# A state space scan followed by an ELU feed-forward block: the last pieces of w_out, the first border's words and the fourth piece of w_in in another order

## The chip, the cores and the metric

The kernel runs on one core of one Trainium2 chip. The core has five engines with instruction queues of their own: TensorE (PE in the profile, with its weight loads shown as PEld), VectorE (DVE), ScalarE (ACT), GpSimd (POOL) and SyncE (SP), which here only starts transfers. Each works through its queue in order, and they wait for one another by semaphores. The metric is the time of one execution on the device, in microseconds (us); the median of several runs counts.

## What is computed

The reference, cut to what matters:

```python
# x (4, 8, 768, 32), a (4, 8, 768), B and C (4, 8, 768, 16); chunks of 32 tokens
cum = np.cumsum(log_a[chunk])
M = (C @ B.T) * exp(cum_i - cum_j) * causal      # per batch and head
y = M @ x + (C @ state) * exp(cum)
state = exp(sum(log_a)) * state + sum_j B_j x_j exp(cum_last - cum_j)
# y of (b, h, s, d) becomes X of (b*s, h*d) = (3072, 256)
h = X @ w_in                                     # (3072, 2048)
g = where(h > 0, h, exp(min(h, 0)) - 1)
out = g @ w_out                                  # (3072, 256)
```

The two weight matrices arrive as 64-bit floating point numbers and are turned into 32-bit ones on the chip; everything else is in 32 bits.

## The kernel before, in words

**Blocks.** The 3072 tokens are twelve blocks of 256, numbered n = 0 to 11. Blocks 0 to 3 are treated one at a time, later ones in pairs (2 and 3 together from the middle of the kernel on, then 4 and 5, and so on). For each block the scan part makes y: `turn_square` and `turn_part` turn B and C (VectorE), `mask_heads` (line 457) makes the masked copies of C, `turn_exp` scales C (VectorE, line 444), `scaled` scales B (GpSimd, line 408), `decay` makes the decay factors (ScalarE, then a select on GpSimd, lines 521 and 526), `scores`, `sums`, `across` and `inside` are small products on TensorE (lines 541, 571, 616, 634), `weigh` and `states` work on their results (VectorE, lines 550 and 588, with a GpSimd product at 593). `inside` ends with copies to `yT` on ScalarE (line 651), in two halves, `ts` 0 and 1.

**Weights.** `pieces` lists sixteen pieces: 0 to 7 are eight column slices of w_in, 8 to 15 are pairs of row slices of w_out. A piece is made by `w_abs` (ScalarE, line 196), `w_low` (ScalarE, line 205, or VectorE, line 209), `w_sign` (VectorE, line 223), `w_high_a` (a clamp on VectorE, line 231), `w_high_b` (VectorE, line 238) and `w_sum` (GpSimd, line 248). `w_high` is the two high steps, `w_take` the first three, `w_give` the others. Pieces are numbered so that w_out's last, 15, is what the eighth step of the second product of block 0 reads, `l2(0, 7)`.

**Products.** Blocks 0 to 3 use full 32-bit products for part of the work: `l1(n, i)` (line 667) for x times w_in, and `l2(n, j)` (line 829) for g times w_out; `elu` follows `l1`. From column slice 8 of blocks 2 and 3 on, `l1_words(n, m)` (line 787) takes three faster passes over words: high words `w1` with `y1`, low words `w0` with `y0`, and sums of words `both_w` with `both_y`. `words_of_w(p)` makes w1 and both_w of piece p on ScalarE and VectorE (lines 736, 737), and `low_of_w(p)` makes w0 on GpSimd (two subtractions, line 845). `words_of_y(n)` makes y1 (lines 755, 757, 759) and y0 (line 762), `both_of_y(n)` makes both_y (line 772, VectorE). After its passes a slice goes through ScalarE (line 793), VectorE (796), ScalarE twice (802, 803, in `begin_end`) and VectorE again (810, in `end_words`, one slice later). `m` counts slices, and slice m reads piece m // 2.

**The second product of pairs.** `second` (line 904) multiplies g by w_out for two blocks with seven products in place of eight. It needs sums of quarters of w_out: `differences` and `sum_weights` make them on GpSimd (lines 845 and 714), `sum_t1` and `sum_t2` make those of g. `differences(i, count)` reads a quarter that `sum_weights` of the same index overwrites.

**Order.** The order of work is written out by hand: an engine's queue holds its instructions in the order of the calls. The stretch that the change touches is, after the first blocks, a loop over j from 0 to 7 (lines 1173 to 1221), in which blocks 2 and 3 take their first slices beside `l2(0, j)` and the last w_out pieces are made (11 at j = 0, 12 to 15 at j = 2 to 5), and a loop over j from 8 to 15, with i = j - 8 (lines 1222 to 1269), in which `l1_words(2, j)` runs beside `l2(1, ...)`. The *first border* is the change from `l1` to `l1_words` at j = 8; the next one is `l1_words(4, 0)`, which follows the second loop. Lines 1270 to 1277 stand between them. PSUM holds seven banks that all these products share (`p_a`) and one more (`p_o`) for `l2` and part of `second`.

The order of the three passes, the one place where the code says more than a sentence:

```python
for ps, lhs, rhs in passes if n > 2 and m == 0 or m == 15 else passes[2:] + passes[:2]:
```

So the sums of words go first, but last for slice 15 and for slice 0 of blocks 4 and later.

Of the kernel before, what the change touches and what calls it, by code (L numbers as in the profile page):

```python
# [32 lines left out]
def kernel(  # L33
# [27 lines left out]
    nc = tc.nc  # L61
# [153 lines left out]
    def w_sign(i, cols=slice(None), eng=nc.vector):  # L215
        if i not in w_sgn:
            w_sgn[i] = ffn.tile([P, 2, CW], U32, tag="g1", name="sgn", bufs=12)
        if eng is nc.gpsimd:
            eng.tensor_scalar(
                out=w_sgn[i][:, :, cols], in0=w_words(i)[1][:, :, cols].bitcast(mybir.dt.int32),  # L220
                scalar1=0.0, scalar2=2.0 ** 31, op0=ALU.is_lt, op1=ALU.mult)
            return
        nc.vector.tensor_scalar(
            out=w_sgn[i][:, :, cols], in0=w_words(i)[1][:, :, cols], scalar1=0x80000000,
            scalar2=None, op0=ALU.bitwise_and)
# [16 lines left out]
    def w_high(i):  # L242
        w_high_a(i)
        w_high_b(i)
# [213 lines left out]
    def mask_heads(n):  # L458
        s = st[n]
        s["ctm"] = att.tile([P, 2, 2, P], F32, tag="ctm", name="ctm")  # L460
        nc.vector.tensor_tensor(
            out=s["ctm"], in0=s["ct"].unsqueeze(2).to_broadcast([P, 2, 2, P]),
            in1=hmask2.unsqueeze(1).unsqueeze(3).to_broadcast([P, 2, 2, P]), op=ALU.mult)
# [218 lines left out]
    def elu():  # L682
        if not begun:
            begin_elu()
        n, i, ps = lag.pop(0)
        e = begun.pop()
        nc.scalar.activation(e, e, ACT.Exp, scale=-1.0)  # L687
        g_of[n, i] = ffn.tile([P, 2, BLK], F32, tag=f"g{n % 2}", name="g", bufs=12)
        nc.vector.scalar_tensor_tensor(
            out=g_of[n, i], in0=e, scalar=1.0, in1=ps,  # L690
            op0=ALU.subtract, op1=ALU.max)
# [39 lines left out]
    def words_of_w(i):  # L731

        w = pieces[i][0]
        k_words[i] = conv.tile(
            [P, 2, KC, CW], F32R, tag="w64", name="w_words", bufs=W_AHEAD)
        nc.scalar.activation(k_words[i][:, 0], w, ACT.Copy, scale=NEAR)
        nc.vector.scalar_tensor_tensor(
            out=k_words[i][:, 1], in0=k_words[i][:, 0].bitcast(F32), scalar=1.0 / WORD - 1.0,
            in1=w, op0=ALU.mult, op1=ALU.add)
# [10 lines left out]
    def words_of_y(n):  # L750

        y = yT[n // 2].rearrange("p k b u i -> p k (b u i)")
        y1 = conv.tile([P, KC, 2 * BLK], F32R, tag="y1", name="y1", bufs=1)
        y0 = conv.tile([P, KC, 2 * BLK], F32R, tag="y0", name="y0", bufs=1)
        nc.scalar.activation(y1[:, 1], y[:, 1], ACT.Copy, scale=NEAR / WORD)
        if n == 4:
            nc.scalar.activation(y1[:, 0], y[:, 0], ACT.Copy, scale=NEAR / WORD)
        else:
            nc.vector.tensor_scalar(
                out=y1[:, 0], in0=y[:, 0], scalar1=NEAR / WORD, scalar2=None, op0=ALU.mult)  # L760
        for k in range(KC):
            nc.vector.scalar_tensor_tensor(  # L762
                out=y0[:, k], in0=y1[:, k].bitcast(F32), scalar=WORD, in1=y[:, k],
                op0=ALU.mult, op1=ALU.subtract)
        y_words[n] = y1, y0

    def both_of_y(n):
        y = yT[n // 2].rearrange("p k b u i -> p k (b u i)")
        y1, y0 = y_words[n]
        both = ffn.tile([P, KC, 2 * BLK], F32R, tag="yT", name="y_both")  # L770
        for k in range(KC):
            nc.vector.scalar_tensor_tensor(  # L772
                out=both[:, k], in0=y1[:, k].bitcast(F32), scalar=1.0 - WORD,
                in1=y[:, k], op0=ALU.mult, op1=ALU.add)
        y_words[n] = y1, y0, both

    def l1_words(n, m, between=None):

        cols = slice(m % 2 * P, (m % 2 + 1) * P)
        w, w0 = k_words[m // 2]  # L780
        w1, both_w, w0 = w[:, 0, :, cols], w[:, 1, :, cols], w0[:, :, cols]
        y1, y0, both_y = y_words[n]
        high, both = psum([P, 2 * BLK], "ps_h"), psum([P, 2 * BLK], "ps_w")
        passes = [(high, w1, y1), (high, w0, y0), (both, both_w, both_y)]
        for ps, lhs, rhs in passes if n > 2 and m == 0 or m == 15 else passes[2:] + passes[:2]:
            for k in range(KC):
                nc.tensor.matmul(  # L787
                    out=ps, lhsT=lhs[:, k], rhs=rhs[:, k], start=k == 0 and lhs is not w0,
                    stop=k == KC - 1 and lhs is not w1)
        if between:  # L790
            words_of_y(between)
        e = ffn.tile([P, 2 * BLK], F32, tag="e", name="e", bufs=2)
        nc.scalar.activation(e, both, ACT.Copy, scale=WORD)  # L793
        if late:
            end_words()
        nc.vector.scalar_tensor_tensor(  # L796
            out=high, in0=high, scalar=WORD - 1.0, in1=e, op0=ALU.mult, op1=ALU.add)
        late.append((n, m, high, e))
# [167 lines left out]
    def w_take(i, low):  # L966

        w_abs(i)
        w_low(i, low)
        w_sign(i)  # L970

    def w_give(i):

        w_high(i)
        w_sum(i)
# [71 lines left out]
    w_abs(3)  # L1047
    w_low(3, nc.scalar)
    w_sign(3)
    mask_heads(1)  # L1050
    w_high(3)
    turn_b(1)
    nc.scalar.activation(F[:, 1], F[:, 0], ACT.Exp)
    write_flat_exp()
# [36 lines left out]
    todo = 5  # L1091
# [77 lines left out]
    def differences(i, count):  # L1169
        for r in range(i, i + count):  # L1170
            sub(s_out[1][:, r], a_out[0][:, r], a_out[2][:, r])

    for j in range(2 * DIRECT):
        n, i = 2 + j // DIRECT, j % DIRECT
        if j < 7:
            l2(0, j)
        piece = todo < len(pieces) and j != 1
        if j == 0:
            elu()
        if piece:  # L1180
            w_take(todo, nc.vector)
        l1(n, i)
        if j == 7:
            l2(0, j)
        if j == 0:
            scaled(3, nc.gpsimd)
            turn(3)
            elu()
            turn_exp(3)
        if piece:  # L1190
            w_give(todo)
            todo += 1
        while lag:
            elu()
        if j == 0:
            decay(3, 2)
            decay(3, 3)
        if j == 1:
            scores(3)
            sums(3)  # L1200
            for q in range(4):
                weigh(3, q)
        if j == 2:
            states(3)
        if j == 3:
            inside(across(3), 3)
        if j == 4:
            words_of_y(2)
        if j == 4:
            words_of_w(4)  # L1210
        if j == 5:
            low_of_w(4)
        if j == 5:
            both_of_y(2)
        scan_ahead(j)
        if j == 3:
            s_out[:] = weight_sums()
        if j == 6:
            differences(0, 4)
        if j == 7:  # L1220
            words_of_w(5)
    for j in range(8, 16):
        i = j - 8
        l1_words(2, j, between=4 if i == 7 else None)
        for p in ((), (6,), (), (7,), (0,), (1,), (2,), ())[i]:
            words_of_w(p)
        for p in ((5,), (), (6,), (7,), (0,), (), (), ())[i]:
            low_of_w(p)
        if i == 7:
            l2(1, 6)  # L1230
            l2(1, 7)
        begin_end()
        if i == 0:
            turn_part(5, 2)
            scaled(4, nc.gpsimd)
            scaled(5, nc.gpsimd)
        if i < 2:
            load_bc(i + 6)
            l2(1, i)
        if i == 2:  # L1240
            turn_part(4, 3)
            turn_part(5, 3)
            scores(4, 5)
            sums(4, 5)
            for q in range(4):
                weigh_two(4, q)
            l2(1, 2)
            states(4)
            states(5)
            for to in (6, 7):  # L1250
                load_b(to)
                spread_cum(to)
        if i == 3:
            l2(1, 3)
        if i == 4:
            y = across(4, 5)
            inside(y, 4, 5, ts=(0,))
            l2(1, 4)
            inside(y, 4, 5, ts=(1,))
        if i == 5:  # L1260
            l2(1, 5)
        if i in (0, 1, 3, 4):
            sum_t1(2, (0, 1, 3, 4).index(i), nc.vector)
        if i in (4, 6):
            turn_part(6, i // 2 - 2)
        if i in (2, 5):
            differences(4 if i == 2 else 6, 2)
        if i < 6:
            sum_weights(nc.gpsimd, a_out, s_out, i)
    both_of_y(4)  # L1270
    end_words()
    words_of_w(3)
    decay(6, 0)
# [107 lines left out]
```

## Time and profile before

| What | Value |
|---|---|
| Time, median of 3 runs | 350.4 us (350.18 to 352.61) |
| Profiled execution, its own time | 349.9 us |
| Its span, from the first to the last instruction | 348.1 us |
| TensorE clock granted, mean | 0.999 |
| TensorE busy, in the stretch from 30 to 80 us | all of it but 0.02 us |
| TensorE busy, from 80 to 88, 88 to 96, 96 to 104, 104 to 112, 112 to 120 us | 7.17, 7.70, 8.00, 7.54, 7.32 of 8 us each |
| VectorE busy, from 88 to 104 us | 15.8 of 16 us |
| GpSimd busy, from 80 to 112 us | 30.6 of 32 us |

The span leaves out 1.8 us of the execution's own time. Times in the text are from the span's start. A row of the timeline has the start of a group of like instructions, how long it lasted, the engine, the line, the operation, what it writes and reads, the shapes and how many there were; in brackets the idle time of the engine before it and what ended that.

### The profile page before, as it was taken

The page shows a single profiled execution, that of the slowest core. Times are in us where ns is not written, and L with a number is a line of the kernel's source. Part 1 is how long each engine was busy: PE and PEld are TensorE (multiplying, and loading weights), DVE is VectorE, ACT ScalarE, POOL GpSimd, SP SyncE. Part 2 cuts the span into 40 slices and gives each one's busy share as a digit, 9 for nine tenths or more (in the row PEclk, how much of TensorE's full clock was granted, in tenths as well). Part 3 has the DMA queues.
Part 4 walks back from the last instruction along what each step waited for, and adds up shares of the span by engine and source line. Part 5 has one row for each costly group of instructions (what it writes and reads, how often), then busy time and mean ns, then how long its engine had stood idle before and what let it go on. Part 6 is the DMA issues. An engine that isn't in the chain of part 4 may idle for free.

```text
span 348.1 us, 9872 instructions
## 1 busy us (share of the span) xinstructions
PE 339.8 (98%) x3878; PEld 297.9 (86%) x3878; DVE 258.7 (74%) x515; ACT 235.3 (68%) x537; POOL 217.1 (62%) x338
## 2 busy tenths in 40 slices
PE   8899999999999999999999999999999999999996
PEld 5679888887777799988988988988988999999995
DVE  3998979879996889775878675888675756665232
ACT  5789989697658889647699447699557566565000
POOL 5654554557999499984196864196854174455760
PEclk9999999999999999999999999999999999999999
DMA  8987979471350321080431070330000100001002
GB/s 135 262 206 166 295 153 263 88 150 45 69 135 8 93 61 33 6 160 7 104 64 32 6 151 15 91 49 2 2 0 5 62 0 3 0 0 62 3 0 62
DMA packets 72727, 26.49 MB, mean 76 GB/s; under 512 B 57768, under 2 KB 67560, under 8 KB 72680
## 3 DMA queue, kind: packets, MB, share of 16 engines
q1 hardware_dynamic: 70360, 25.60, 31.6%
q8 instruction: 30, 0.49, 0.6%
q10 hardware_dynamic: 2320, 0.26, 0.5%
q14 instruction: 17, 0.14, 0.1%
HBM read 22.51 MB, written 3.34 MB: 74 GB/s over the span
## 4 chain that ended last, share of the span: by engine, by line
PE 83%; ACT 4%; DVE 3%; POOL 3%; SPq 2%; issue 2%; DMA 1%; POOLq 0%; DVEq 0%; ACTq 0%
PE ps_o L904 36%; PE ps_h L787 18%; PE ps_w L787 9%; PE ps_h L667 9%; PE ps_o L829 4%; PE ps_y L634 2%; PE ps_g L541 2%; DMA w<-in_moe_w_in_dram 1%; PE ps_y L616 1%; PE ps_st L571 1%; POOL L L526 1%; POOL w L845 1%; ACT e L687 1%; DVE y L762 1%; SPq L178 1%
## 5 line engine op out<-in xcount | busy, mean ns | idle before, releaser
L904 PEld LDWEIGHTS ps_o<-w_out,g 128*128 128x128 f32 x640 | 78.5, 191 | 3.4
L904 PE MATMUL ps_o<-w_out,g 128*128 128x128 f32 x640 | 80.1, 275 | 0.0
L802 ACT ACTIVATE e<-ps_h 128x512 f32<-128x512 f32 x72 | 43.0, 598 | 50.4 <-DVE ps_h L796 50.4
L810 DVE SCALAR_TENSOR_TENSOR g<-e,ps_h 128x512 f32<-128x512 f32 x72 | 49.4, 686 | 30.3 <-ACT e L803 29.8
L845 POOL TENSOR_TENSOR g<-g 128x256 f32<-128x256 f32 x36 | 26.6, 739 | 55.5 <-DVE g L810 55.5
L796 DVE SCALAR_TENSOR_TENSOR ps_h<-ps_h,e 128x512 f32<-128x512 f32 x72 | 50.1, 695 | 13.2 <-ACT e L793 10.1
L793 ACT ACTIVATE e<-ps_w 128x512 f32<-128x512 f32 x72 | 42.3, 588 | 15.0 <-PE ps_w L787 14.9
L787 PE MATMUL ps_w<-y_both,w_words 128*128 128x512 f32 x144 | 51.4, 436 | 0.7 <-DVE y_both L772 0.6
L803 ACT ACTIVATE e<-e 128x512 f32<-128x512 f32 x72 | 45.5, 633 | 2.3
L667 PE MATMUL ps_h<-yT,w_in 128*128 128x256 f32 (+1 forms) x208 | 45.1, 367 | 1.6 <-POOL w_in L248 1.1
L787 PE MATMUL ps_h<-y,w_words 128*128 128x512 f32 x144 | 45.8, 399 | 0.0
L787 PE MATMUL ps_h<-y,w 128*128 128x512 f32 x144 | 44.9, 392 | 0.2 <-POOL w L845 0.2
L667 PEld LDWEIGHTS ps_h<-yT,w_in 128*128 128x128 f32 x208 | 36.4, 190 | 7.2 <-POOL w_in L248 2.3
L521 ACT ACTIVATE L<-L,ncum 128x64 f32<-128x64 f32 x160 | 42.3, 337 | 0.3
L904 PE MATMUL ps_o<-w_sum,g 128*128 128x128 f32 x304 | 38.3, 275 | 0.0
L904 PEld LDWEIGHTS ps_o<-w_sum,g 128*128 128x128 f32 x304 | 37.1, 192 | 1.1
L526 POOL TENSOR_SCALAR_AFFINE_SELECT L<-L 64x512 f32<-64x512 f32 x40 | 29.2, 730 | 9.7 <-ACT L L521 8.3
L787 PEld LDWEIGHTS ps_h<-y,w 128*128 128x128 f32 x144 | 27.0, 188 | 6.9 <-POOL w L845 0.7
L845 POOL TENSOR_TENSOR g<-t,g 128x256 f32<-128x256 f32 x40 | 28.2, 738 | 5.8 <-PE ps_o L904 5.7
L787 PEld LDWEIGHTS ps_h<-y,w_words 128*128 128x128 f32 x144 | 26.4, 188 | 5.9 <-issue 0.5
L829 PE MATMUL ps_o<-w_out,g 128*128 128x256 f32 x128 | 30.6, 383 | 0.8 <-POOL w_out L248 0.8
L845 POOL TENSOR_TENSOR g<-g,t 128x256 f32<-128x256 f32 x40 | 28.8, 754 | 0.2
(133 smaller groups left out, 538.2 us busy)
## 6 DMA issues: line engine op xcount, KB each, us to landing
L<-flat SPq DMA_DIRECT2D x20, 256.0 KB
w<-in_moe_w_out_dram SPq DMA_DIRECT2D x8, 512.0 KB
w<-in_moe_w_in_dram SPq DMA_DIRECT2D x7, 512.0 KB
xr<-in_x_dram SPq DMA_DIRECT2D x24, 128.0 KB
out_dram<-c_sum SPq DMA_DIRECT2D x9, 256.0 KB
bc<-in_B_dram SPq DMA_DIRECT2D x24, 64.0 KB
bc<-in_C_dram SPq DMA_DIRECT2D x22, 64.0 KB
ec<-flat_exp SPq DMA_DIRECT2D x10, 128.0 KB
```

Of the source, the lines that this page charges most:

```text
L521: nc.scalar.activation(L[:, h, u], L[:, h, u], ACT.Exp, bias=ncum[:, u, row:row + 1])
L526: nc.gpsimd.affine_select(out=part, in_=part, pattern=[[0, 4], [0, 2], [1, Q]], compare_op=ALU.is_ge, fill=0.0, base=0, channel_multiplier=-1)
L667: nc.tensor.matmul(out=ps[:, j, toks], lhsT=w_in[i][:, k, j * P:(j + 1) * P], rhs=yT[n // 2][:, k, n % 2].rearrange("p u i -> p (u i)")[:, ...
L787: nc.tensor.matmul(out=ps, lhsT=lhs[:, k], rhs=rhs[:, k], start=k == 0 and lhs is not w0, stop=k == KC - 1 and lhs is not w1)
L793: nc.scalar.activation(e, both, ACT.Copy, scale=WORD)
L796: nc.vector.scalar_tensor_tensor(out=high, in0=high, scalar=WORD - 1.0, in1=e, op0=ALU.mult, op1=ALU.add)
L802: nc.scalar.activation(e, high, ACT.Relu, scale=-1.0)
L803: nc.scalar.activation(e, e, ACT.Exp, scale=-1.0)
L810: nc.vector.scalar_tensor_tensor(out=g_of[n, m].rearrange("p b i -> p (b i)"), in0=e, scalar=1.0, in1=h, op0=ALU.subtract, op1=ALU.max)
L829: nc.tensor.matmul(out=o_of[n][:, ts], lhsT=g_of[n, j][:, m % 2, ts * P:(ts + 1) * P], rhs=w_out[:, m], start=(m == 0 and ts == 0), stop=( ...
L845: nc.gpsimd.tensor_tensor(out=out, in0=in0, in1=in1, op=ALU.subtract)
L904: nc.tensor.matmul(out=ps[:, ts], lhsT=b[:, ts * P:(ts + 1) * P], rhs=a[:, i], start=(i == chunk[0] and ts == 0), stop=(i == chunk[-1]), s ...
```

## The change

`w_high(3)`, the clamp and the second high step of w_in's fourth piece, goes ahead of `mask_heads(1)`. Piece 15 is made at the end of j = 4 in place of j = 5, with its low step on ScalarE in place of VectorE. For blocks 2 and 3 one half of y1 is made by ScalarE in place of VectorE; for blocks 4 and 5 by VectorE in place of ScalarE. Slice 8 takes its sums of words last. The differences of w_out's quarters are spread over i = 0, 2, 3 and 5 in place of j = 6 and i = 2 and 5. `low_of_w(5)` moves from i = 0 to j = 7. The second half of `inside` for blocks 4 and 5 moves from i = 4 to the middle of `l2(1, 5)`. `both_of_y(4)` moves from behind the loop to directly behind `words_of_y(4)`, which is ahead of the ScalarE and VectorE steps of slice 15.

```diff
         nc.scalar.activation(y1[:, 1], y[:, 1], ACT.Copy, scale=NEAR / WORD)
-        if n == 4:
+        if n == 2:
             nc.scalar.activation(y1[:, 0], y[:, 0], ACT.Copy, scale=NEAR / WORD)
         else:
...
-        for ps, lhs, rhs in passes if n > 2 and m == 0 or m == 15 else passes[2:] + passes[:2]:
+        for ps, lhs, rhs in passes if m == (8 if n == 2 else 0) or m == 15 else passes[2:] + passes[:2]:
...
         if between:
             words_of_y(between)
+            if between == 4:
+                both_of_y(4)
...
     w_sign(3)
+    w_high(3)
     mask_heads(1)
-    w_high(3)
     turn_b(1)
...
         while lag:
             elu()
+        if j == 4:
+            w_take(todo, nc.scalar)
+            w_give(todo)
+            todo += 1
...
-        if j == 6:
-            differences(0, 4)
         if j == 7:
             words_of_w(5)
+            low_of_w(5)
...
-        for p in ((5,), (), (6,), (7,), (0,), (), (), ())[i]:
+        for p in ((), (), (6,), (7,), (0,), (), (), ())[i]:
             low_of_w(p)
...
             l2(1, 4)
+        if i == 5:
+            l2(1, 5, half=0)
             inside(y, 4, 5, ts=(1,))
-        if i == 5:
-            l2(1, 5)
+            l2(1, 5, half=1)
...
-        if i in (2, 5):
-            differences(4 if i == 2 else 6, 2)
+        if i in (0, 2, 3, 5):
+            differences((0, 0, 2, 4, 0, 6)[i], 2)
         if i < 6:
             sum_weights(nc.gpsimd, a_out, s_out, i)
-    both_of_y(4)
     end_words()
```

## Prediction before the run

> **What bounds the kernel now.** I read the page's busy shares and its chain first, then the timeline of the weight loads, where TensorE's idle time is given with its releaser, then the other engines' timelines around each idle stretch.
>
> ```profile
> span 348.1 us, 9872 instructions
> PE 339.8 (98%) x3878; PEld 297.9 (86%) x3878; DVE 258.7 (74%) x515; ACT 235.3 (68%) x537; POOL 217.1 (62%) x338
> PE 83%; ACT 4%; DVE 3%; POOL 3%; SPq 2%; issue 2%; DMA 1%; POOLq 0%; DVEq 0%; ACTq 0%
> ```
>
> TensorE is the bound. A reordering that leaves its work as it is can gain no more than its pauses, so I looked for those beside the edits:
>
> ```profile
> 22.53 1.59 PEld L667 LDWEIGHTS ps_h<-yT,w_in 128*128 128x128 f32 x8 [0.65 <-POOL w_in L248]
> 24.45 0.67 PEld L616 LDWEIGHTS ps_y<-bct,Sx 32*64 32x64 f32 x24 [0.33 <-POOL Sx L593]
> ...
> 81.62 1.59 PEld L829 LDWEIGHTS ps_o<-w_out,g 128*128 128x128 f32 x8 [1.23 <-POOL w_out L248]
> ...
> 91.24 0.19 PEld L787 LDWEIGHTS ps_h<-y,w 128*128 128x128 f32 x1 [0.51 <-POOL w L845]
> ...
> 104.95 0.58 PEld L634 LDWEIGHTS ps_y<-M,xr 64*32 64x32 f32 x50 [0.61 <-issue]
> ...
> 116.72 0.19 PEld L787 LDWEIGHTS ps_w<-y_both,w_words 128*128 128x128 f32 x1 [1.01 <-DVE y_both L772]
> 117.32 0.19 PEld L787 LDWEIGHTS ps_w<-y_both,w_words 128*128 128x128 f32 x1 [0.41 <-DVE y_both L772]
> ```
>
> The reader is to see five places, each the consumer of something that the diff moves. From 26 to 80 us and from 118 us on TensorE shows no pause of note.
>
> **The change part by part.** Negative is a gain.
>
> *Piece 15.* l2(0, 7) should follow 16 products of line 667 that begin at 77.17 at 0.216 each, so at 80.63; it begins at 81.62: 0.99 lost to w_sum(15).
>
> ```profile
> 78.36 0.41 DVE L209 TENSOR_SCALAR w_out<-w 128x512 f32<-128x512 uint32 x1
> 80.30 1.27 POOL L248 TENSOR_TENSOR w_out<-mag,w_out 128x512 uint32<-128x512 uint32 x1 [2.88 <-DVE mag L238]
> 80.66 2.58 DVE L772 SCALAR_TENSOR_TENSOR y_both<-y,yT 128x512 fp32r<-128x512 f32 x2
> ```
>
> Moved to j = 4, its steps start behind the elu on VectorE at 73.49: about 74.1 plus sign 0.33, clamp 0.45, shift 0.61 puts w_sum at 75.6 and its end at 76.9, before 80.6. ScalarE gets a low step (0.75) and half of y1 (0.6), 1.35 in all; it has 2.34 us of idle time before its ob copy at 83.65 to hide that. VectorE is relieved of a low step and of y1's half (1.01). Next late would be both_y, which ends at 83.24 while slice 8 begins at 83.27; with y1's second half from ScalarE at 75.8, y0 ends at 77.5, both_y between 80.5 and 81.7, and slice 8 now reads it last, after 82.8. So the 0.99 goes whole: -0.99.
>
> *low_of_w(5) and the differences.* Slice 10 waits for w0 of piece 5: its second low pass begins 0.63 after the first, and what follows 0.43 after that (91.67), where such steps take 0.23: 0.60 lost. GpSimd did four differences (2.16) and a select ahead. Now low_of_w(5) follows the select directly and ends near 88.5, where TensorE asks after 90: -0.60. The differences cost GpSimd the same 2.16, later, two by two (0.9 to 1.3); it starts that stretch some 2.8 earlier, so its sums still end by 113.7. Price at nothing; if that cover were gone, each pair would put 0.9 on low_of_w(7), which ends at 105.35 for a slice at 108.67.
>
> *inside, second half.* It pauses after 13 of 64 at 104.28 and goes on at 104.95; the small products come at 0.007 each, so 0.6 is lost, with no semaphore behind it. Between the two halves lay 1.73 us of l2; now lie 1.73 of l2, a slice (1.4) and half of l2 (0.87). Bounds 0 (the pause moves along) and -0.6; I take -0.6, since the later borders, with 1.98 between the halves, show none.
>
> *both_y(4).* Slice (4, 0) has its high passes done at 115.98 and leaves at 117.66, with 0.47 of work: 1.2 lost, 1.1 without the usual start-up. -1.1 if both_y comes in time.
>
> Sum of TensorE's pauses: 0.99 + 0.60 + 0.60 + 1.1 = 3.3. Two things are late next.
>
> *First border.* ScalarE's order there is unchanged, and VectorE's elu at 21.48 waits for it, so the states, their product Sx and `across` at 24.45 can't come sooner: the 0.65 ahead of l1(0, 3) turns into waiting at 24.45. Gain 0. It can lose:
>
> ```profile
> 18.58 0.81 POOL L408 TENSOR_TENSOR sc<-bc,eb 128x256 f32<-128x256 f32 x1
> 18.83 1.11 DVE L461 TENSOR_TENSOR ctm<-bct,hmask 128x512 f32<-128x512 f32 x1
> 20.92 0.42 DVE L444 TENSOR_TENSOR bct<-bct,ec 128x256 f32<-128x256 f32 x1
> 21.15 1.33 POOL L248 TENSOR_TENSOR w_in<-mag,w_in 128x512 uint32<-128x512 uint32 x1 [1.76 <-DVE mag L238]
> ```
>
> The masked copies took 1.11 beside `sc`, 0.68 elsewhere: 0.43 lost to an operation of GpSimd. In the new order w_sum(3) becomes ready during the masked copies and takes 1.28 just as turn_exp is due; turn_exp ran ahead of it before. Ends: 0, and 1.0 (turn_exp from 20.9 to 22.5, elu at 22.46 in place of 21.48). I take the 0.43 of the one row less the 0.14 that VectorE is free between turn_exp's end at 21.34 and the elu: +0.3, carried through 26 to 80, where nothing absorbs it.
>
> *The words of y for block 4.* The net shift into the second loop is s = 0.99 - 0.3 = 0.7.
>
> ```profile
> 105.66 1.15 ACT L651 COPY yT<-ps_y 128x256 f32<-128x256 f32 x3 [0.31 <-PE ps_y L634]
> 106.83 0.60 ACT L793 ACTIVATE e<-ps_w 128x512 f32<-128x512 f32 x1
> ...
> 117.28 0.61 ACT L736 ACTIVATE w_words<-w_in 128x512 fp32r<-128x512 f32 x1
> ```
> ```profile
> 111.77 0.64 DVE L453 STREAM_TRANSPOSE bct<-bc 128x256 f32<-128x256 f32 x1
> 113.58 1.29 DVE L762 SCALAR_TENSOR_TENSOR y<-y,yT 128x512 fp32r<-128x512 f32 x2 [1.17 <-ACT y L757]
> 115.38 0.69 DVE L796 SCALAR_TENSOR_TENSOR ps_h<-ps_h,e 128x512 f32<-128x512 f32 x1
> 115.98 1.28 DVE L772 SCALAR_TENSOR_TENSOR y_both<-y,yT 128x512 fp32r<-128x512 f32 x2
> ```
>
> VectorE is full from 88 to 105 and moves with s. The yT copies no longer hold back slice 13 on ScalarE, but slice 14; all less s: the first half's copies to 105.3, line 793 to 105.85, VectorE's 796 at 105.95 (it was 107.46), lines 802 and 803 to 107.8, the second half's copies (1.15) to 108.95, line 793 to 109.5, line 796 of slice 14, words of piece 2 and the transpose (0.6 each) to 111.35, where it was 112.41. From there y1's half, two y0, two both_y and one end_words lie ahead of slice 15's step of line 796. Uncontended they take 0.33 + 1.2 + 1.2 + 0.6 = 3.3, contended (1.01, 1.75, 1.6) 5.0; I take 4.3, as GpSimd runs only short sums (0.46) there. Line 796 then starts at 115.65 - s, against 115.38: 0.43 sooner. Behind it are queued lines 802 and 803, words_of_w(3) on ScalarE, and low_of_w(3), (1), (2) on GpSimd. The fourth of those six subtractions ended at 121.79 and what follows slice (4, 2)'s last pass began at 123.08; loaded as late as possible, as at 91.24, that pass could have let it begin at 121.84 + 0.43 = 122.27. That leaves 0.8 of slack. So TensorE can gain 0.8 + 0.43 = 1.2 there, whatever it gained before: of 3.3 - 0.3 = 3.0, another 1.8 turns into a wait at slice (4, 2).
>
> Sum: -1.2. On the profiled execution's own 349.9 that is 348.7; the median of the runs shown is 0.5 above it, so 349.2.
>
> **The rivals.** (a) *Every pause goes.* No loss at the first border (s = 1.0) and line 796 at 114.7 - s: 0.8 + 0.68 + 1.0 = 2.5, so 347.9. For it: turn_exp ran unhindered beside the start of w_sum. Against: VectorE's rows of 0.85 to 1.2 next to GpSimd. 0.20.
>
> (b) *The first border costs its whole 1.0.* GpSimd, waiting since mid-mask, goes first, and turn_exp stands behind a whole w_sum. Then s = 0, line 796 is at 115.65, and the gain is 0.8 - 0.27 = 0.5: 349.9. For it: the two both_y at 80.66 took 2.58 in place of 1.28, as if taking turns with w_sum(15) and low_of_w(4). Against: one row only, of 0.43. 0.20.
> The Trainium skill says this outright (SBUF — State Buffer, "SBUF: two separate sides"): VectorE with two operands in SBUF and GpSimd reading SBUF share a port pair by exclusive lock, held for the whole instruction. The trace agrees as far as the 1.11 beside 0.68; that GpSimd wins the pair here, no run shows. By that rule alone the time would be that of this rival.
>
> (c) *PSUM holds slice 13 back, and it is slower.* The second half of `inside` now keeps two banks through l1_words(2, 13). If that slice gets the banks that the first half's yT copies free, at 105.36 - s, it starts at 104.7, not 102.7; behind it come a slice, l2's halves and `inside` (1.5 + 0.87 + 1.4 + 0.87), so slice 14 starts at 109.3 in place of 108.67. Its high product ends at 110.8; from there line 796 of slice 14, the words of piece 2 and the transpose (1.9) and the 4.3 put line 796 of slice 15 at 117.0, 1.6 later, and slice (4, 2) loses 1.6 - 0.8 = 0.8: 351.2. It decides once line 796 is later than 116.2. For it: before, slice 13 began at 105.62, after those copies, so the trace can't exclude it. Against: slices 11 and 12 free two banks sooner (by 102.4). 0.12.
>
> **How the numbers follow.** The forecast has 0.42, (a) 0.20, (b) 0.20, (c) 0.12; 0.06 is left for what I did not see, on both sides. The forecast's own range is 348.0 to 350.3 (the ends of line 796, 114.7 - s and 116.3 - s, with s between 0.2 and 0.9). The range for 8 in 10 is 347.5 to 350.9: it takes in (b) and most of (a), and stops short of (c). About 1%, 3.5 us, is what a measurement of this kernel can tell from no change. A gain of that size exceeds all pauses (3.3), and only the worst end of (c) with a loss at the first border comes near the other side: faster 0.05, same 0.90, slower 0.05.
>
> **What would show it.** Right: no idle at l2(0, 7), at slice 10's w0 or in `inside`; l1(0, 3) starting near 22.2 and `across` waiting for Sx until 24.7 or so; a new wait of TensorE on GpSimd's line 845 at slice (4, 2). Wrong: `across` at 24.45 or before (then (a)), turn_exp longer than 1 us (then (b)), an idle stretch ahead of slice 13 (then (c)), or no wait at (4, 2), which would say that the last step of this sum is too strict.

## The result, and the profile after

The changed kernel takes 351.3 us (median of 22 runs, 350.79 to 352.16) against 350.34 (22 runs, 349.12 to 352.61): a ratio of 1.0028, 95% interval 1.0018 to 1.0037. That is 0.96 us slower, where a gain of 1.2 was forecast, and it lies above the predicted range, 347.5 to 350.9. It is less than the 1% that the prediction set as the least that can be told from no change; the interval of 22 runs on either side tells 0.28% from no change, so that bound was too coarse. The profiled execution has a time of its own of 350.81 us.

The page after, the same three lines:

```profile
span 349.1 us, 9876 instructions
PE 339.0 (97%) x3878; PEld 297.6 (85%) x3878; DVE 259.3 (74%) x514; ACT 235.1 (67%) x538; POOL 220.0 (63%) x338
PE 77%; ACT 8%; DVE 7%; SPq 2%; issue 2%; DMA 2%; POOL 1%; DVEq 0%; POOLq 0%; ACTq 0%
```

TensorE does the same work, but holds 77% of the chain in place of 83%; ScalarE and VectorE have risen. The timeline of TensorE after, at the places that the prediction looked at and wherever it waited next (the line numbers quoted from 793 on are 2 higher than before):

```profile
23.34 1.97 PE L667 MATMUL ps_h<-yT,w_in 128*128 128x256 f32 x8 [0.90 <-DVE g L689]
25.41 0.88 PE L616 MATMUL ps_y<-bct,Sx 32*64 32x64 f32 x24
...
81.45 1.89 PE L831 MATMUL ps_o<-w_out,g 128*128 128x256 f32 x8
...
92.50 0.85 PE L571 MATMUL ps_st<-xr,b_tok 64*32 64x64 f32 x48 [0.41 <-POOL w_sum L847]
...
120.78 0.49 PE L787 MATMUL ps_h<-y,w 128*128 128x512 f32 x1 [0.28 <-POOL w L847]
121.91 0.50 PE L787 MATMUL ps_h<-y,w 128*128 128x512 f32 x1 [0.63 <-POOL w L847]
...
146.00 0.84 PE L571 MATMUL ps_st<-xr,b_tok 64*32 64x64 f32 x56 [0.43 <-DVE c_sum L884]
```

The reader is to see: `l2(0, 7)` at 81.45 without a wait, and slice 10 and `inside` without one too. `across` is at 25.41 in place of 24.45. The pause at slice (4, 0), 1.01 and 0.41 on the weight loads before, is 0.50 once on them, and too short for a mark on the products. New are 0.41 at `sums` of blocks 4 and 5 (GpSimd's differences), 0.28 and 0.63 at slice (4, 2), and 0.43 at `sums` of blocks 6 and 7, which wait for VectorE.

**How executions are compared.** Single executions start unevenly: `w_abs(2)` (line 196 on ScalarE), the first step that waits for the transfer of piece 2, begins between 14.56 and 16.10 us in the profiles of this case. So below I count places in a profile from that start. Of the 0.96 by which `across` is later in the rows above, 0.39 is such a late start (14.96 for 14.57). Two profiles of the kernel before then agree within 0.2 us at the places of the next table; between 105 and 116 us they differ by 0.4.

### The profile page after: what moved, and what is told of

The parts are those of the page before. It is cut to its first block, busy times and chain, and to the rows that moved or that the text cites. A ratio compares the mean times of both kernels' runs of the same rounds, so it can differ in the third digit from the quotient of the medians.

```text
span 349.1 us, 9876 instructions
## 1 busy us (share of the span) xinstructions
PE 339.0 (97%) x3878; PEld 297.6 (85%) x3878; DVE 259.3 (74%) x514; ACT 235.1 (67%) x538; POOL 220.0 (63%) x338
## 3 DMA queue, kind: packets, MB, share of 16 engines
HBM read 22.51 MB, written 3.34 MB: 74 GB/s over the span
## 4 chain that ended last, share of the span: by engine, by line
PE 77%; ACT 8%; DVE 7%; SPq 2%; issue 2%; DMA 2%; POOL 1%; DVEq 0%; POOLq 0%; ACTq 0%
PE ps_o L906 31%; PE ps_h L787 15%; PE ps_h L667 10%; PE ps_w L787 8%; PE ps_o L831 5%; PE ps_y L634 2%; DVE ps_h L798 2%; ACT L L521 2%; DMA w<-in_moe_w_in_dram 2%; ACT e L804 2%; PE ps_y L616 2%; ACT e L805 1%; PE ps_st L571 1%; ACT e L795 1%; PE ps_g L541 1%
## 5 line engine op out<-in xcount | busy, mean ns | idle before, releaser
L847 POOL TENSOR_TENSOR g<-g 128x256 f32<-128x256 f32 x36 | 27.3, 757 | 56.0 <-DVE g L812 55.9
L526 POOL TENSOR_SCALAR_AFFINE_SELECT L<-L 64x512 f32<-64x512 f32 x40 | 29.9, 746 | 9.9 <-ACT L L521 8.5
```

Source lines behind the costliest of these rows:

```text
L526: nc.gpsimd.affine_select(out=part, in_=part, pattern=[[0, 4], [0, 2], [1, Q]], compare_op=ALU.is_ge, fill=0.0, base=0, channel_multiplier=-1)
L847: nc.gpsimd.tensor_tensor(out=out, in0=in0, in1=in1, op=ALU.subtract)
```

## The experiments

The theories, as the expectations name them. *W*: the prediction's own, `low_of_w(1)` at slice (4, 2) sets the end. *V*: from slice 15 on VectorE's queue, with ScalarE's, sets the pace, and what goes ahead of line 798 there is paid. *Q*: the loss is there by 25 us, from the transfer of piece 2 on. *P*: it lies in late pauses, and at the last store. *L*: `turn_exp` is shut out for as long as one instruction of GpSimd runs; *N* is anything else at that place. *First border* in the prediction and below is the stretch from 19 to 25 us, from block 0 to block 1 (not the change from `l1` to `l1_words`).

All results in one table. Places are in us from the start of `w_abs(2)`, of one profile each; "end" is the stretch from the start of the last product to the end of the span; "DVE" is the number of instructions on VectorE, semaphore instructions counted.

| Kernel | Median, us | Ratio to before, 95% interval | DVE | turn_exp | across | 796/798 of slice 15 | last product | end |
|---|---|---|---|---|---|---|---|---|
| before | 350.34 | 1 | 707 | 0.42 | 9.89 | 100.81 | 329.97 | 3.60 |
| ctl_before | one run | | 707 | 0.42 | 9.70 | 100.71 | 330.08 | 3.41 |
| after | 351.30 | 1.0028 (1.0018 to 1.0037) | 706 | 1.32 | 10.46 | 100.50 | 330.03 | 4.09 |
| ctl_after | one run | | 706 | 1.31 | 10.44 | 100.53 | 329.70 | 4.46 |
| before_border | 351.30 | 1.0022 (1.0010 to 1.0034) | 708 | 1.31 | 10.55 | 101.50 | 330.85 | 3.34 |
| after_border_back | 350.65 | 0.9999 (0.9984 to 1.0014) | 705 | 0.43 | | | | 3.48 |
| after_sum_halves | 350.71 | 1.0016 (1.0006 to 1.0027) | 706 | 0.77 | 9.90 | 99.94 | 329.49 | 4.20 |
| after_y_back | 350.33 | 0.9994 (0.9980 to 1.0008) | 705 | 1.31 | 10.45 | 99.56 | 329.76 | 3.50 |
| both_back | 349.07 | 0.9960 (0.9945 to 0.9974) | 704 | 0.42 | 9.72 | 98.57 | 328.62 | 3.27 |
| border_order_back | 348.51 | 0.9950 (0.9938 to 0.9961) | 705 | 0.42 | 9.70 | 98.04 | 328.11 | 3.50 |
| border_order_back_w3 | 349.50 | 0.9972 (0.9960 to 0.9985) | 705 | 0.42 | 9.67 | 98.02 | 328.94 | 3.49 |
| after_w3 | 350.51 | 1.0003 (0.9993 to 1.0013) | 706 | 1.31 | 10.44 | 100.61 | 329.89 | 4.08 |
| after_three_sets | 350.37 | 0.9991 (0.9979 to 1.0004) | 708 | 1.31 | 10.45 | 100.58 | 329.84 | 3.31 |
| border_order_back_two_sets | 349.74 | 0.9969 (0.9955 to 0.9983) | 706 | 0.42 | 9.70 | 98.04 | 328.09 | 4.08 |
| grid_neither | 348.50 | 0.9920 (0.9908 to 0.9932) | 708 | 0.42 | 9.72 | 98.10 | 327.91 | 3.34 |
| grid_border | 349.24 | 0.9948 (0.9935 to 0.9961) | 708 | 1.31 | 10.46 | 98.85 | 328.65 | 3.36 |
| grid_y | 349.32 | 0.9952 (0.9940 to 0.9964) | 708 | 0.42 | 9.80 | 99.84 | 329.09 | 3.56 |
| grid_both | 350.72 | 0.9995 (0.9982 to 1.0009) | 708 | 1.31 | 10.44 | 100.57 | 329.69 | 3.46 |

The profile of after_border_back was taken at a granted clock of 0.994, so its places are left out. Each group of runs had its own runs of the kernel before beside it, and their medians go from 350.32 to 351.08. So a ratio is to the kernel before of the same group, and medians from different groups can't be compared to better than some 0.8 us. The groups are: before and after; the next row with after_border_back, after_y_back and both_back; after_sum_halves with border_order_back, its w3 version and after_w3; the two "sets"; and the four of the grid.

### The first border

`before_border`, the swap alone, in the kernel before:

```diff
+    w_high(3)
     mask_heads(1)
-    w_high(3)
```

> The kernel before, with only the clamp and shift of w_in's fourth piece put ahead of the masked copies. Theory V: turn_exp waits for w_sum and takes 1.3, across comes 0.7 later, TensorE is 0.7 later up to 80 us and slice 15's step starts near 116.1 in place of 115.38: 351.0, 0.7 over the kernel before. Theories Q and P: 350.3, no change.

`after_border_back`, the swap taken out of the changed kernel:

> The changed kernel, with the clamp and shift of w_in's fourth piece back behind the masked copies. Theory V (VectorE's queue): turn_exp runs in 0.42 again in place of 1.31, the states and across come 0.7 sooner, slice 15's step after its passes (line 798 there) starts near 114.8 in place of 115.46, and all behind it moves along: 350.6, 0.7 under the changed kernel's 351.3. Theory Q (the late first border comes from a late transfer of piece 2 in the one profiled execution): no change, 351.3. Theory P (the loss is TensorE's short pauses late in the kernel, at 145, 205 and 213, and the last store): no change, 351.3.

The swap alone costs 0.22% (0.8 us), and the last product comes 0.8 to 0.9 us later, counted from a step by which the transfer of piece 2 has landed: it is the swap's own loss, and not a late transfer's, as Q would have it. In the changed kernel, taking it out gains 0.29% (0.9999 for 1.0028), about 1.0 us; as its end is 0.6 to 1.0 shorter (below), this run alone doesn't show the border's share. VectorE's timeline after, and GpSimd's:

```profile
19.10 0.75 DVE L231 TENSOR_SCALAR mag<-mag 128x512 f32<-128x512 f32 x1
19.89 0.69 DVE L238 SCALAR_TENSOR_TENSOR mag<-mag,sgn 128x512 uint32<-128x512 uint32 x1
20.50 0.68 DVE L461 TENSOR_TENSOR ctm<-bct,hmask 128x512 f32<-128x512 f32 x1
21.29 1.32 DVE L444 TENSOR_TENSOR bct<-bct,ec 128x256 f32<-128x256 f32 x1
22.52 0.67 DVE L689 SCALAR_TENSOR_TENSOR g<-e,ps_h 128x512 f32<-128x512 f32 x1
```
```profile
20.73 1.59 POOL L248 TENSOR_TENSOR w_in<-mag,w_in 128x512 uint32<-128x512 uint32 x1 [1.15 <-DVE mag L238]
```

`turn_exp` (line 444) takes 1.32 in place of 0.42: `w_sum(3)` began while the masked copies ran (20.50 to 21.18), and `turn_exp` ends 0.29 behind its end (22.61 and 22.32). The elu comes at 22.52 in place of 21.48, and TensorE's `l1(0, 3)` waits for it. To tell whether that is one instruction's length, `after_sum_halves` splits the sum:

```diff
-    w_sum(3)
+    w_sum(3, ks=slice(0, 1))
+    w_sum(3, ks=slice(1, 2))
```

> The changed kernel, with w_sum(3) on GpSimd made in two halves of 0.65 in place of one operation of 1.28. Theory L (turn_exp, with both operands in SBUF, is shut out while one GpSimd instruction runs): VectorE gets in between the halves, turn_exp takes 0.7 or so in place of 1.31, across comes 0.6 sooner, and the time falls by 0.6: 350.7, ratio 1.0011. Rival N (turn_exp is late for another reason, or GpSimd keeps its turn through both halves): turn_exp still takes 1.3 or more, ratio 1.0028.

```profile
21.38 0.77 DVE L444 TENSOR_TENSOR bct<-bct,ec 128x256 f32<-128x256 f32 x1
```
```profile
20.82 1.92 POOL L248 TENSOR_TENSOR w_in<-mag,w_in 128x256 uint32<-128x256 uint32 x2 [1.15 <-DVE mag L238]
```

`turn_exp` now ends at 22.15, before GpSimd's second half does (22.74) and 0.28 behind the end of its first half (21.87), as it ended 0.29 behind the whole sum above. `across` is 0.56 sooner (9.90 for 10.46). So it is shut out for one instruction of GpSimd at a time: L. The Trainium skill states this (SBUF — State Buffer, "SBUF: two separate sides": the shared port pair is an exclusive lock, held for the whole instruction by whichever started first), and the 1.32, 0.77 and 0.42 agree. That GpSimd, which was already waiting, got in ahead of `turn_exp` is what these runs add.

### The words of y for block 4

`after_y_back` puts `both_of_y(4)` back behind the loop, and block 4's half of y1 back on ScalarE; `both_back` undoes the border as well:

```diff
-        if n == 2:
+        if n in (2, 4):
...
-            if between == 4:
-                both_of_y(4)
...
+    both_of_y(4)
     end_words()
```

> The changed kernel, with the words of y for block 4 as before: both halves of y1 on ScalarE, and the sums of words of y behind the loop, so behind slice 15's step. Theory V: slice 15's step starts near 114.0 in place of 115.46; TensorE waits about 1.2 for the sums of words at slice (4, 0), but no longer 1.35 at slice (4, 2); VectorE's queue is 1.4 earlier from there on and TensorE no longer waits at the sums of blocks 6 and 7: 350.3 to 350.7, 0.6 to 1.0 under the changed kernel. Theory P: 351.3.

> The changed kernel with both of these put back: the fourth piece's clamp and shift behind the masked copies, and the words of y for block 4 as before. Theory V: the two gains add, slice 15's step near 113.3: 349.5 to 350.0, below the kernel before by 0.3 to 0.8. Theory Q: as the version with the words of y alone. Theory P: 351.3.

after_y_back has 350.33 (0.9994), in the range that V gave, but not for V's reason alone. Line 796 of slice 15 comes 0.9 sooner (99.56 for 100.50, where 1.5 was expected), and the waits at slice (4, 2) and at the sums of blocks 6 and 7 are gone. Yet its last product, at 329.76, is 0.27 sooner than in one profile of the changed kernel and 0.06 later than in the other, while its end is 0.6 to 1.0 shorter: most of what its time gained lies at the end. both_back, at 349.07 (0.9960), gained more than expected; its last product is 1.1 to 1.4 sooner than the changed kernel's.

`border_order_back` is both_back with y1's half left on VectorE, so that only the two orders are undone. `border_order_back_w3` calls `words_of_w(3)` at i = 7 on top of that, and `after_w3` does so in the changed kernel:

```diff
-        for p in ((), (6,), (), (7,), (0,), (1,), (2,), ())[i]:
+        for p in ((), (6,), (), (7,), (0,), (1,), (2,), (3,))[i]:
             words_of_w(p)
...
     end_words()
-    words_of_w(3)
```

> The changed kernel with the first border put back, and the sums of words of y for block 4 put back behind the loop, but y1's first half for block 4 left on VectorE. It parts the two edits that went back together in the version at 0.996. Theory V: VectorE starts y0 0.8 sooner than in that version, where it waited 1.22 for ScalarE's y1; slice 15's step and the sums of words each come some 0.6 sooner: ratio 0.994, 0.6 us under that version. Rival: the half on VectorE costs what the wait did; ratio 0.996.

> The same, and words_of_w(3) called at i = 7, ahead of slice 15's last steps on ScalarE, in place of behind the loop. Theory V (VectorE and ScalarE pace each other from slice 15 on): ScalarE's queue is 0.5 shorter there, at most 0.5 of gain: ratio 0.993 to 0.994. Theory W (the prediction's: low_of_w(1) on GpSimd, which follows words_of_w(3), sets the end at slice (4, 2)): no wait is left at (4, 2) in the version without this edit, so no gain: ratio as that one.

> The changed kernel, with words_of_w(3) called at i = 7, so that low_of_w(3), (1) and (2) start 2 us or more sooner. Both theories: TensorE's wait of 1.35 at slice (4, 2) goes. Theory W: that wait was what ate the gain, so the time falls by about 1.3: 350.0, ratio 0.999. Theory V: TensorE is stopped later by VectorE's queue (at the sums of blocks 6 and 7, 0.6), which gains only the 0.5 that ScalarE is rid of: 350.8, ratio 1.0014.

With both orders undone the rest of the change gains 0.40 to 0.50%: border_order_back, at 0.9950, beats both kernels. Against both_back its line 796 of slice 15 and its last product are 0.5 sooner (98.04 for 98.57, 328.11 for 328.62), as V expected of y1's half on VectorE; the two ratios, of different groups, don't tell them apart.

after_w3 has 1.0003, between what W and V expected, so the time doesn't decide. Its profile does: it has no wait at slice (4, 2) any more, but its last product comes at 329.89, where the changed kernel's two profiles have 330.03 and 329.70. The wait turned up later, most of it at the sums of blocks 6 and 7 (145.97, 0.58 of TensorE's idle time, for a result of VectorE). So W is out: the wait at (4, 2) isn't the last limit.

border_order_back_w3 missed both expectations: V had a gain, W no change, and the last product came 0.8 later. Line 796 of slice 15 is where it was (98.02 for 98.04); the extra word step of VectorE delays both_y instead, and TensorE's pause for it at slice (4, 0) goes from 0.38 to 1.19. So VectorE's time was paid there too, but through both_y and not, as V has it, through the step of slice 15.

### The end of the program

The changed kernel's last product, so counted, came no later than before, yet the medians differ by 0.96. Two second profiles:

> The kernel before, unchanged, for a second profile of it. Read from the start of w_abs(2) on ScalarE (line 196, the first step that waits for piece 2's transfer), the first profile had `across` at 9.89 us, line 796 of slice 15 at 100.81 and the last product at 329.97. If single profiles read in this way can be trusted to 0.3 us, this one has 9.6 to 10.2, 100.5 to 101.1 and 329.7 to 330.3. If they scatter as much as the kernels differ, the last is off by 0.6 or more.

> The changed kernel, unchanged, for a second profile of it. Read in the same way the first profile had `across` at 10.46 us, line 798 of slice 15 at 100.50 and the last product at 330.03, that is only 0.06 later than the kernel before, where the medians say 0.96. If the difference is scatter of the two single profiles, this one has its last product at 330.6 to 331.2. If it lies behind the last product (the last store) or ahead of w_abs(2), the last product comes at 329.8 to 330.3 again, and the span beyond it is longer than that of the kernel before by some 0.5.

The last product comes at 329.70, and the rest takes 4.46 (4.09 in the first profile), against 3.60 and 3.41 before: the changed kernel loses 0.5 to 1.0 us behind its last product. In the records of the transfers, the last load of instructions (queue 14) begins 1.8 and 2.2 us behind the last product's start, within the last store; before it is at 1.1 and 0.9. In all profiles the place of that load, and the end, went by the number of instructions on VectorE, which the change had altered by one. So I altered that number alone, at 1.05 us, where VectorE has idle time behind it; `after_three_sets`:

```diff
-    nc.vector.memset(keep, 1.0)
+    nc.vector.memset(keep[:, 0, 0:64], 1.0)
+    nc.vector.memset(keep[:, 0, 64:128], 1.0)
+    nc.vector.memset(keep[:, 1], 1.0)
```

> The changed kernel, but the memset of line 272 on VectorE (at 1.05 us, with 1.8 us of idle time behind it) in three parts, so VectorE's queue is two instructions longer and nothing else is moved. In all profiles so far the stretch from the start of the last product to the end of the span went by the number of instructions on VectorE, semaphore instructions counted: 707 or 708, 3.35 to 3.60 us (the kernel before among them); 706, 4.08 to 4.46 (the changed kernel, twice, and two of its variants); 704 or 705, 3.27 to 3.50. In the same profiles a load of instructions (queue 14) lies at 0.9 to 1.1 us behind that start, at 1.8 to 2.2, within the last store, or at 3.8 to 4.1. Theory T (the load of VectorE's last block of instructions holds up the last store where the two meet): with 708 the stretch takes 3.3 to 3.6 again, and the time is 0.5 to 0.8 lower than the changed kernel's 351.3: 350.5 to 350.8, a ratio of 1.0005 to 1.0015. The rival (the longer end has to do with the change itself, or is chance): 4.1 to 4.5 again, and 351.3.

`border_order_back_two_sets` does the same in two parts, `keep[:, 0]` and `keep[:, 1]`:

> The version that has been the fastest (border and both_of_y(4) in their old order), but the memset of line 272 in two parts: one instruction more on VectorE, 706 in place of 705. Theory T: the load of instructions falls on the last store, the stretch behind the last product's start takes 4.1 to 4.5 in place of 3.5, and the time rises from 348.5 by 0.6 to 0.9: a ratio of 0.997 in place of 0.995. The rival: 3.5 and 0.995 again.

The end went from 4.09 and 4.46 to 3.31, and from 3.50 to 4.08, as expected of theory T. It holds in all 18 profiles: with 706 instructions the end takes 4.08 to 4.46 (five profiles), with 704, 705, 707 or 708 it takes 3.27 to 3.60 (thirteen). The last packet of the store (queue 1) is over 2.50 to 2.87 behind the last product's start in the five, and 1.90 to 2.12 in the others. The last store's issue, in the SyncE timelines after, of after_three_sets, of border_order_back and of its two_sets version, each under the answer's own line with the span:

```profile
core 0 of [0], span 349.1 us
...
345.68 0.35 SPq L898 DMA_DIRECT2D out_dram<-c_sum  x1
```
```profile
core 0 of [0], span 347.8 us
...
345.20 0.35 SPq L900 DMA_DIRECT2D out_dram<-c_sum  x1
```
```profile
core 0 of [0], span 346.7 us
...
343.92 0.35 SPq L896 DMA_DIRECT2D out_dram<-c_sum  x1
```
```profile
core 0 of [0], span 346.7 us
...
343.35 0.35 SPq L897 DMA_DIRECT2D out_dram<-c_sum  x1
```

From issue to end: 3.4, 2.6, 2.8 and 3.35. And the transfers behind that issue after (the window from 346.6 to 348.6):

```profile
q1 hardware_dynamic: 124, 0.06, 9.6%
q14 instruction: 1, 0.01, 1.7%
```

The store's packets and one load of instructions share that window; in after_three_sets both late loads are over by then, and its window from 346.2 to 347.6 has queue 1 alone. The Trainium skill (Runtime: NRT & Kernel Launch, "Instruction fetch mechanics") has instruction fetch hidden behind the issuing of instructions, and speaks there of the engine's own issue and not of other transfers; here the end was 0.6 to 1.2 us longer where a load met the last store. Theory P, which looked to the last store, was right in this part. That the load delays the store is an inference from both tests; what in the load does it isn't shown.

The times fit in part: border_order_back_two_sets has 0.9969 (expected 0.997); after_three_sets has 0.9991, lower than expected (1.0005 to 1.0015). These are ratios of different groups of runs, so the two orders are measured side by side below, with ends alike.

### Two by two

Four kernels in one group, all brought to 708 instructions on VectorE (the memset in three or four parts): with both parts, with only `both_of_y(4)` early, with only the swap at the border, and with neither. The rest of the change is in all four.

> The changed kernel with VectorE's queue brought to 708 instructions (the memset of line 272 in three parts), so that its end can be compared with the other three of this group, brought to the same number: a two-by-two of the two parts that were found to cost time, with the difference at the end of the program taken out. This one has both parts. From its first measurement: a ratio of 0.9991, between 0.998 and 1.0005. Theory A (the two losses add): 0.2 to 0.35 per cent above each of the two with one part. Theory M (each of them alone makes a limit, and the larger of the two counts): the same as the one with both_of_y(4) early alone.

> w_high(3) behind mask_heads(1) as before, both_of_y(4) early as in the changed kernel, 708 instructions on VectorE. Theory A: 0.9965 to 0.998, with the border's loss of 0.2 to 0.35 per cent gone from the one with both. Theory M: the same as with both, 0.9985 to 1.0005, TensorE arriving sooner at slice (4, 2) and waiting there for longer.

> w_high(3) ahead of mask_heads(1) as in the changed kernel, both_of_y(4) behind the loop as before, 708 instructions on VectorE. Theory A: 0.996 to 0.998. Theory M: 0.9975 to 0.9995, the loss of 0.3 per cent at the first border above the one with neither part, and within 0.1 per cent of the one with both.

> Both parts in their old order, the rest of the change kept, 708 instructions on VectorE. Both theories: 0.9945 to 0.996, as measured with 705. That is the gain of the rest of the change, 1.4 to 1.9 us.

Above "neither", the border adds 0.74 us and the words of y 0.82, both together 2.2 (medians); by the last product 0.74, 1.18 and 1.78. The sum of the two single losses is 1.56 by the medians and 1.92 by the last product, so they add, roughly, as theory A says, and M, by which the words of y alone would cost as much as both, is out. The ratios themselves missed both theories: the three versions that lack a part came 0.1 to 0.3% lower than either had them, and the gap between both parts and one is 0.43 to 0.47%, where A had 0.2 to 0.35. In the profiles the border's loss is there from `across` on and stays (0.74 at both ends). TensorE's waits in grid_neither, then in grid_y, from 76 to 150 us:

```profile
92.33 0.85 PE L574 MATMUL ps_st<-xr,b_tok 64*32 64x64 f32 x48 [0.42 <-POOL w_sum L848]
114.91 0.50 PE L790 MATMUL ps_w<-y_both,w_words 128*128 128x512 f32 x1 [0.31 <-DVE y_both L775]
115.77 0.50 PE L790 MATMUL ps_w<-y_both,w_words 128*128 128x512 f32 x1 [0.36 <-DVE y_both L775]
```
```profile
92.18 0.85 PE L574 MATMUL ps_st<-xr,b_tok 64*32 64x64 f32 x48 [0.41 <-POOL w_sum L850]
120.45 0.50 PE L790 MATMUL ps_h<-y,w 128*128 128x512 f32 x1 [0.28 <-POOL w L850]
121.59 0.51 PE L790 MATMUL ps_h<-y,w 128*128 128x512 f32 x1 [0.63 <-POOL w L850]
145.69 0.84 PE L574 MATMUL ps_st<-xr,b_tok 64*32 64x64 f32 x56 [0.44 <-DVE c_sum L887]
```

The waits for both_y at slice (4, 0), 0.67 together, go in grid_y, and three others come, 1.35 together. VectorE's timelines of the two, up to the step of slice 15 (line 799, then 801, the 796 of before):

```profile
111.16 1.89 DVE L765 SCALAR_TENSOR_TENSOR y<-y,yT 128x512 fp32r<-128x512 f32 x2
112.98 0.68 DVE L813 SCALAR_TENSOR_TENSOR g<-e,ps_h 128x512 f32<-128x512 f32 x1
113.57 0.69 DVE L799 SCALAR_TENSOR_TENSOR ps_h<-ps_h,e 128x512 f32<-128x512 f32 x1
114.17 1.54 DVE L775 SCALAR_TENSOR_TENSOR y_both<-y,yT 128x512 fp32r<-128x512 f32 x2
```
```profile
110.98 1.89 DVE L765 SCALAR_TENSOR_TENSOR y<-y,yT 128x512 fp32r<-128x512 f32 x2
112.80 1.81 DVE L775 SCALAR_TENSOR_TENSOR y_both<-y,yT 128x512 fp32r<-128x512 f32 x2
114.53 0.68 DVE L815 SCALAR_TENSOR_TENSOR g<-e,ps_h 128x512 f32<-128x512 f32 x1
115.12 0.69 DVE L801 SCALAR_TENSOR_TENSOR ps_h<-ps_h,e 128x512 f32<-128x512 f32 x1
117.14 0.69 DVE L815 SCALAR_TENSOR_TENSOR g<-e,ps_h 128x512 f32<-128x512 f32 x1 [1.33 <-ACT e L808]
```

Moving both_y ahead buys TensorE 0.92 (its end: 100.24, then 99.32) and pushes the step of slice 15 back by 1.74 (98.10, then 99.84). Behind that step stands a ring in which VectorE and ScalarE wait for each other. In grid_y VectorE waits for ScalarE's line 808 six times between 115 and 145 us (0.25 to 1.33), and ScalarE for VectorE's line 801 seven times (0.27 to 1.76). The last rounds of it, and the adds to `c_sum` for which TensorE waits at the sums of blocks 6 and 7, first in grid_y, with a row of ScalarE, then in grid_neither:

```profile
143.26 0.69 DVE L815 SCALAR_TENSOR_TENSOR g<-e,ps_h 128x512 f32<-128x512 f32 x1 [1.07 <-ACT e L808]
144.80 0.74 DVE L887 TENSOR_TENSOR c_sum<-ps_o,c_sum 128x256 f32<-128x256 f32 x2
```
```profile
144.59 0.60 ACT L807 ACTIVATE e<-ps_h 128x512 f32<-128x512 f32 x1 [0.95 <-DVE ps_h L801]
```
```profile
143.42 0.74 DVE L885 TENSOR_TENSOR c_sum<-ps_o,c_sum 128x256 f32<-128x256 f32 x2
```

Counted from `w_abs(2)` (15.28 and 15.48 in these two profiles) the adds start at 129.52 and 127.94: of the 1.74 at slice 15, 1.58 is still there 30 us later. TensorE shows no wait between 122 and 145 us, so it isn't TensorE that holds the ring up.

## Why the prediction was wrong, step by step

How far TensorE is ahead of the kernel before (mean of its two profiles, counted from `w_abs(2)`) at the start of what is named, in us; negative is sooner, and "after" is the first profile of the changed kernel:

| Place (time before) | neither | border | y | both | after |
|---|---|---|---|---|---|
| across (24.6) | -0.04 | +0.71 | +0.05 | +0.69 | +0.71 |
| l2(0, 7) (81.6) | -1.17 | -0.41 | -1.13 | -0.41 | -0.48 |
| slice 10, second low pass (91.2) | -1.76 | -1.00 | -1.72 | -1.02 | -1.07 |
| sums of 4 and 5, behind their wait (93.0) | -1.57 | -0.81 | -1.54 | -0.82 | -0.88 |
| slice (4, 0), second pass over both_y (117.3) | -2.41 | -1.66 | -3.32 | -2.60 | -2.67 |
| slice (4, 2), behind its wait (122.8) | -2.38 | -1.64 | -1.93 | -1.21 | -1.28 |
| sums of 6 and 7, behind their wait (146.0) | -2.29 | -1.54 | -1.04 | -0.32 | -0.39 |
| a product of blocks 10 and 11 (308.9) | -2.14 | -1.40 | -0.91 | -0.31 | -0.02 |

- *Piece 15 (0.99) and low_of_w(5) (0.60)*: right in place and about in size, 1.1 and 0.6 (first column). The differences, priced at nothing, cost 0.2 at the sums of 4 and 5, where the row after names one of them as what ended the wait.
- *inside (0.60)*: the pause is gone, but its size was one execution's: between the same two products the second profile of before has 0.37 in place of 0.67. Nor are this pause and the next one separate terms: in that profile TensorE waits 0.29 longer for both_y at slice (4, 0) (0.87 for 0.58 on the products).
- *First border (+0.3)*: **mis-sized**. It cost 0.74, and rival (b)'s mechanism was right: GpSimd, waiting during the masked copies, goes first, and `turn_exp` stands behind what is left of w_sum. I took the one row with 0.43 (a VectorE step beside `sc`) less 0.14 of slack, and not the whole instruction that was about to start.
- *l1(0, 3) near 22.2*: wrong. It was at 23.34, as its first product waits for an elu, which stands behind `turn_exp`.
- *Words of y, line 796 sooner by 0.43*: a consequence of s. With s = 1.17 - 0.74 = 0.43, and not 0.7, the same sum (115.65 - s) gives 0.16 sooner; it came 0.2 sooner (100.50 to 100.58 for 100.76). What I put between the transpose and line 796 (4.3, of bounds 3.3 and 5.0) is 4.5 after (110.95 to 115.46).
- *The cap of 1.2 at slice (4, 2)*: right in its mechanism, and in its number partly by luck. TensorE was 2.6 ahead and is 1.2 to 1.3 ahead behind that wait. But line 796 was 0.2 sooner and not 0.43, and the slack behind it was 1.0 to 1.1 and not 0.8; the two errors cancel.
- *That the 1.2 then lasts to the end*: **the step that failed**. I followed the delay to the first consumer with slack, and not on through VectorE's and ScalarE's ring. VectorE was only 0.2 ahead, and where TensorE next waits for a result of that queue, at the sums of blocks 6 and 7, the lead shrinks from 1.2 to between 0.3 and 0.4: the step put at nothing cost 0.9. The order of before leaves 1.2 us more at that point: the pause of 1.1 at (4, 0) was the price of a queue that is in time later.
- *The end of the program*: a term put at nothing, as the prediction stops at slice (4, 2). It cost 0.5 to 1.0 by the profiles.

Together: the last product is level with before in one profile after and 0.33 ahead in the other; the first loses 0.26 in a pause at 213.49 that the other lacks and for which no releaser is named. The end of the span, counted from `w_abs(2)`, is 334.11 and 334.16 in the two profiles after, 333.57 and 333.49 before: 0.6 slower, of the 0.96 measured. The other 0.4 is ahead of that step or is scatter of single profiles; no run tells which. Rival (b) had the border right, but its 349.9 shares the last two errors. Rival (a) is out, since the waits came back; so is (c), as TensorE is busy for all of the 16 us from 96 to 112 after.

What stays open: ratios of different groups scatter more than their intervals say. The version with neither part has 0.9950 with 705 instructions and 0.9920 with 708, at ends and last products that agree within 0.2 us. Its own medians agree too, 348.51 and 348.50; what differs is the kernel before beside it, 350.32 and 351.08, on the same chip. Why that one moves isn't settled. Within a group the order of the versions holds, but sizes by median and by last product differ by up to 0.4 us.

## What to carry to other kernels

Before an operation is moved ahead of a step that runs in a ring of two engines, follow that step's delay through every later place where the bottleneck needs a result of the ring: a pause that TensorE loses at one border can be the cheaper one. Take a pause from two profiles before it is priced, and when two kernels differ by less than 0.3%, look at the stretch behind the last product first. A VectorE step with two SBUF operands that becomes due while GpSimd is already waiting should be priced at the whole instruction of GpSimd: here 0.9 us for one of 1.28.

## What the runs showed of the hardware

- A GpSimd sum that became ready while VectorE ran one product went ahead of VectorE's next one, in all nine profiles with that order: `turn_exp` took 1.31 to 1.32 us in place of 0.42 behind a whole w_sum (eight profiles), and 0.77 behind half of one.
- One or two more small instructions on VectorE at the start of the program moved the end by 0.6 to 1.2 us, both ways (3.50 to 4.08; 4.09 and 4.46 to 3.31), with a load of instructions met by the last store in the long ones.
- The start of an execution is uneven: the first step that waits for piece 2's transfer began between 14.56 and 16.10 us, with no order among the kernels.
